# A one-column activation ahead of table loads, and rows of means and scales stored straight from their columns

## The chip, the core and the metric

The kernel runs on one core of a Trainium2 chip. The metric is device microseconds of one execution, as the median of three runs. Besides its timed runs a kernel has one execution taken by the hardware profiler; all rows below are from that one.

## The reference

One sequence of S = 2048 rows and D = 512 columns, 32 heads of 16, F = 1376, all in float32. `xn` is the layernorm of x; A is a linear attention, B a token mixer with an MLP, and the output gates the one with the other:

```
xn = layernorm(x)
q, k, v = xn @ wqkv                       # 32 heads
phi(t) = where(t > 0, t + 1, exp(t)) + 1e-6
kv = sum_s phi(k) v ;  z = sum_s phi(k)
s  = (phi(q) kv / (phi(q) z + 1e-6)) @ wo
h  = gelu(layernorm(xn) @ w1)
hs = [shift +1, -1, +2, -2 of the quarters of h] @ w2
x1 = xn + hs
B  = x1 + gelu(layernorm(x1) @ w3) @ w4
out = x + s * silu(B)
```

## The kernel before

**Tiling.** Rows go in 16 tiles of 128 (`NT`), or 4 blocks of 512 (`NQ` blocks of `QT` = 4 tiles). Matrix products are made in float32r with each operand split into a rounded part and a rest (tiles that end in h and l), so one product is three matmuls. Many products are made by a scheme of seven products of half matrices (`seven`, `keys_queries`, the pairs `p`, `u`, `pb`, `pe`, `pa`, `gf`), which needs sums of operands before and sums of results after; these are ACT's copies and DVE's additions around every group of matmuls.

**Stages.** First the weights wk, wq and w1 and the 16 tiles of x and of its transpose xt are loaded. For each block, means and variances of the rows are taken from x (BATCH_NORM_STATS2 and BATCH_NORM_AGGREGATE into the columns of `mv1`), keys and queries are projected, features of keys are multiplied with x (`gram`, the products g into G), and the mixer's first product h = w1 times u (`mix1`), u being xt less the mean of each row, is scaled by a row factor (`au`) and goes through gelu. Then come w2, the MLP with w3 and w4 in pairs of 128-column slices (tiles `w_`, `f_`, `gf`, `p`, `pb`), and at the end the queries' features against the attention's matrix (`pbs`, with query tiles in pairs q0/q1 to q14/q15), silu, the gating and the store.

**Rows of means and scales.** The mean and the factor of a row stand in columns, one row of x per partition. `make_u` and `mix1` need them along the free axis, on all partitions. `spread` brings them there: TensorE transposes 128x4 numbers into a PSUM bank (`cb` for means, `ab` for scales), ACT copies the 4x128 result (`cr`, `ar`), SP stores it as four rows of 512 bytes into a row in DRAM (`mrow`, `arow`), and a later DMA reads 512 numbers of that row back to all 128 partitions (`um` in `make_u`, `abc` in `join_a`). It runs seven times: four times for scales, three times for means.

**What sets the order.** Every operation is first only recorded (`Plan.add`), with the engine, a duration and what it reads and writes. `Plan.emit` then issues them one at a time: on each engine it chooses among the operations whose inputs are planned by due time, and puts in estimates for table loads (`TABLE`), DMA landings (`RATE`, by kind of transfer) and buffers that come free. A table of pairs at the end of the program, `SOONER`, moves the due times of single operations by quarters of a microsecond. The emitted order is fixed in the program; what the chip then waits for is set by semaphores. A buffer's next user waits for those who used it last.

**Tables on ACT.** Exp, gelu and silu each need their own table of the ACT engine. When an activation with another table than the last follows, the compiler puts an ACT_TABLE_LOAD in front of it. `Plan.act` (L170) knows the three tables by index, and `emit` adds `TABLE` to the planned start where the index changes.

**Queues.** SP issues the loads and the plain stores, in the order in which the planner emitted them; an SP instruction that waits for a semaphore holds all that stand behind it. POOL issues the DMAs that add into their target (`gather`).

**Names that the steps touch.** `w1m` is the product of ones with the sum of w1's rows (`center`, read from `w1ml`), from which DVE takes the centred weights `w_s`, which ACT rounds into `w_0h`, the operand of the first h. `kt` is DVE's sum over a key bank; `qsum` is a later product in the same bank. `turn_q` makes `pq` (ACT, Exp) from queries; `up_pair` makes the MLP's `gf` from its banks (`pb`, `pe`, `pa`) over the copies `p` and `u` (in the orders below `f_..a` are gelu of gf or of a bank, rounded, `f_..t` and `f_..s` the rounded sums of them, `w_2_0h` the rounded sums of a pair of w3). `xr` are the rows of x which the last tiles are gated into; `q14d` and `q15d` the last two query tiles in DRAM, `q14t` and `q15t` the same read back.

Of the kernel before, what the change touches and what calls it, by code (L numbers as in the profile page):

```python
# [8 lines left out]
F32 = mybir.dt.float32  # L9
# [5 lines left out]
P = 128  # L15
# [11 lines left out]
class Tile:  # L27


    def __init__(self, plan, tag, name, dtype, width, rows=P):  # L30
        self.plan, self.tag, self.name, self.dtype, self.width, self.rows = plan, tag, name, dtype, width, rows
        self.ap = None
        self.log = []
        self.left = 0
        self.end = 0.0
        self.psum = tag in plan.psum
        self.early = plan.early
# [45 lines left out]
class Op:  # L83
    __slots__ = ("eng", "busy", "lat", "emit", "pre", "post", "tiles", "opens", "two", "table", "patience", "soon", "loads",
                 "nom", "due", "ready", "at", "end", "mb", "order", "rate", "tail")


class Plan:
# [9 lines left out]
    def add(self, eng, busy, lat, reads, writes, emit, two=False, table=None, mb=0.0):  # L98
# [3 lines left out]
        op.order = len(self.ops)  # L102
        op.patience, op.soon, op.rate, op.tail = self.patience, False, 0.0, 0.0
        op.loads = any(isinstance(v, View) and v.tile.tag != "dram" for v in writes)
# [29 lines left out]

    last_pe = None

    def soon(self, op):
# [21 lines left out]
    def act(self, out, src, func, scale=1.0, bias=None, total=None):  # L159
# [11 lines left out]

        self.add("ACT", lat - .1, lat, [src, scale, bias], [out] + ([] if total is None else [total]), emit, table=table)

# [48 lines left out]
    def gather(self, out, src, share=1.0, kind="gather"):  # L222
# [3 lines left out]
    RATE = {"load": 2.93, "fetch": 3.3, "half": 4.27, "row": 4.23, "turn": 5.4, "store": 2.45,  # L226
            "gather": 5.73, "quarter": 6.42}

# [9 lines left out]
    DMA0 = 2.2  # L238
    TABLE = 1.41
    TAIL = {"row": .95}  # L240
# [33 lines left out]
    def backward(self):  # L274
        for op in reversed(self.ops):
            if op.eng != "PE":
                for o in op.post:
                    op.due = min(op.due, o.due - self.GAP[o.eng] - (6.0 + op.mb * 4 if op.mb else op.lat))

    def emit(self, first, lead, reserve, window, ahead, table=()):  # L280
        self.deadlines(first)
# [14 lines left out]
        under = [0.0] * 8, [0.0] * 8  # L296
        table = 0
        done = set()
        slip = 0.0
        left = len(ops)  # L300
        while left:
# [5 lines left out]
            for e, cands in avail.items():  # L307
                picks = []
                low = INF
                for op in cands:  # L310
# [7 lines left out]
                    if op.table is not None and op.table != table:  # L318
                        s = max(s, free[e] + self.TABLE)
                    ok = True  # L320
# [24 lines left out]
                    if op.table is not None and op.table != table and op.due + slip < s:  # L345
                        q = s - self.TABLE
                    picks.append((q, s, op))
# [35 lines left out]
            for t in op.tiles:  # L383
                t.left -= 1
                t.end = max(t.end, op.end)
                if not t.left and t.tag in slots:
                    insort(slots[t.tag], (t.end, t.slot))
            for o in op.post:
                flow = o.pre[op]
# [17 lines left out]
def linear_attn_gated_by_mixer(  # L407
# [231 lines left out]

    def spread(name, src, b, row):  # L640

        ps = pl.new("mm", f"{name}b{b}", F32, 512)[:QT, :P]
        pl.transpose(ps, src, ident.all)
        t = pl.new("p", f"{name}r{b}", F32, PIECE)[:QT, :P]
        pl.act(t, ps, AF.Copy)
        pl.store(row.via(lambda ap: ap.rearrange("o (j p) -> (o j) p", p=P)), t)

    def spread_a(b):
        spread("a", au[:, b * QT:(b + 1) * QT], b, arow[:, EDGE + b * BT:EDGE + (b + 1) * BT])

    def spread_m(b):
        spread("c", means(mv1, b * QT, (b + 1) * QT), b, mrow[:, b * BT:(b + 1) * BT])

# [964 lines left out]
    for b in range(NQ):  # L1618
# [82 lines left out]
    SOONER = (  # L1701
# [5 lines left out]
    )  # L1707
# [39 lines left out]
```

## Time and profile before

| | us |
|---|---|
| runs | 508.28, 509.31, 509.06 |
| median of the runs | 509.06 |
| the profiled execution | 507.67 |
| its span, from first to last instruction | 505.9 |

| in the profiled execution | |
|---|---|
| operations recorded on the five engines and their queues | 9830 instructions |
| ACT's instructions | 756, of them 26 ACT_TABLE_LOAD and 7 copies of 4x128 |
| PE's matmuls | 3287, of them 7 transposes of a spread |
| DVE, POOL | 945 and 157 instructions |
| DMA | 90895 packets, 115.67 MB |

A row of the profile's timeline reads: start (us), duration (us), engine, line of the kernel, operation, out<-in by the program's names, shapes, and in brackets the time for which the engine stood before it, with the instruction that ended the wait. A row that ends in x3 stands for three such instructions in a run. In the view of waits a row is: engine, what waited, `<-` its releaser; then the total us, how many, and the longest. In the view by groups, numbers behind the bar are total busy us, mean ns of one, and then idle us before the group, with its releasers. The planner's times and the program's order can't be read as times of the chip.

### The profile page before, as it was taken

Reading aid. Unit: us, or ns where it says so; the run is one execution under the profiler, and the core shown is the slowest. Engines: PE = TensorE matmul, PEld = TensorE weight load, DVE = VectorE, ACT = ScalarE, POOL = GpSimd, SP = SyncE. Lnnn points to the kernel's source line nnn. Section 1 sums busy time; section 2 is a strip of 40 time slices with the busy share of each in tenths; the row PEclk is TensorE's granted clock in tenths of the full one; section 3 lists DMA queues with packets and bytes.
Section 4 is the critical chain, followed back from the end, with each engine's and each line's share of the span. In section 5 each row is a group of like instructions: output and inputs, shape, how many; then the busy total and the mean of one; then the engine's idle time right before and its main releaser. Section 6 shows DMA issues by size and latency. Waiting matters only on the chain.

```text
span 505.9 us, 9830 instructions
## 1 busy us (share of the span) xinstructions
PE 496.0 (98%) x3287; PEld 450.9 (89%) x3287; DVE 439.6 (87%) x945; ACT 375.4 (74%) x756; POOL 110.0 (22%) x157
## 2 busy tenths in 40 slices
PE   8999999999999999999999999999998999999996
PEld 6676878898888888898999989999998999999996
DVE  5899999999699995999999997987878869999464
ACT  5899689666797785967767688857588767997551
POOL 2178303363235222021000020300030300031100
PEclk9999999999999999999999999999999999999999
DMA  7957957359994799889785979998799799899905
GB/s 255 356 127 207 314 180 189 62 123 284 269 336 107 227 293 231 265 215 315 260 261 175 317 249 307 225 227 233 226 230 292 160 235 257 258 232 272 245 3 126
DMA packets 90895, 115.67 MB, mean 229 GB/s; under 512 B 8800, under 2 KB 50044, under 8 KB 90844
## 3 DMA queue, kind: packets, MB, share of 16 engines
q1 hardware_dynamic: 78668, 98.00, 60.8%
q0 software_dynamic: 12176, 17.04, 20.4%
q8 instruction: 26, 0.43, 0.3%
q14 instruction: 25, 0.20, 0.1%
HBM read 73.70 MB, written 32.91 MB: 211 GB/s over the span
## 4 chain that ended last, share of the span: by engine, by line
PE 89%; ACT 6%; DMA 3%; DVE 1%; issue 1%; SPq 1%; ACTq 0%
PE a L148 15%; PE pb L148 11%; PE h L148 9%; PE g L148 7%; PE pbk L148 7%; PE acc L148 6%; PE pe L148 6%; PE pbs L148 4%; PE pbm L148 4%; PE pek L148 3%; PE uc L148 3%; PE pa L148 3%; PE pes L148 2%; PE pem L148 2%; PE pak L148 2%; DMA x<-in_x 1%
## 5 line engine op out<-in xcount | busy, mean ns | idle before, releaser
L224 POOL DMA_DIRECT2D th<-in_x x14 | 15.5, 1392 | 169.6 <-DMA w_t<-w4t 59.8
L170 ACT ACT_TABLE_LOAD x26 | 33.4, 1283 | 4.4 <-issue 1.8
L224 POOL DMA_DIRECT2D e<-x1d x12 | 14.4, 1248 | 58.3 <-DMA q8d<-q8z 20.5
L224 POOL DMA_DIRECT2D o<-x x16 | 14.0, 892 | 43.3 <-DVE o L192 30.9
L170 ACT ACTIVATE gf<-gf 128x256 f32<-128x256 f32 (+1 forms) x48 | 21.8, 466 | 0.5
L224 POOL DMA_DIRECT2D zacc<-kr x16 | 14.2, 887 | 36.0 <-DMA zacc<-kr 20.9
L616 POOL TENSOR_TENSOR rs<-w,nhalf 128x4 f32<-128x4 f32 (+2 forms) x10 | 10.1, 1006 | 34.4 <-DVE w L197 24.4
L170 ACT ACTIVATE ht<-ht 128x512 f32<-128x512 f32 x16 | 9.6, 626 | 7.1 <-DVE ht L192 6.8
L170 ACT ACTIVATE p<-pb 128x256 f32<-128x256 f32 x20 | 7.6, 378 | 9.2 <-PE pb L148 9.2
L610 DVE BATCH_NORM_STATS2 st<-o 128x6 f32<-128x512 f32 x16 | 10.8, 684 | 3.2 <-DMA o<-x 3.2
L192 DVE TENSOR_TENSOR gf<-pa,p 128x256 f32<-128x256 f32 x20 | 8.4, 418 | 6.0 <-PE pa L148 4.0
L192 DVE TENSOR_TENSOR th<-th,so 128x512 f32<-128x512 f32 (+1 forms) x17 | 10.7, 655 | 2.7 <-ACT th L170 2.7
L192 DVE TENSOR_TENSOR e<-a,e 128x512 f32<-128x512 f32 (+1 forms) x12 | 7.6, 662 | 6.2 <-PE a L148 6.2
L170 ACT ACTIVATE x<-x,nm,rs 128x512 f32<-128x512 f32 x16 | 12.8, 808 | 0.0
L202 DVE SCALAR_TENSOR_TENSOR kr<-kt,kr 128x512 f32<-128x512 f32 x16 | 10.9, 686 | 2.1 <-ACT kt L170 2.0
L170 ACT ACTIVATE p<-pe 128x256 f32<-128x256 f32 x20 | 7.7, 384 | 6.2 <-PE pe L148 6.1
L202 DVE SCALAR_TENSOR_TENSOR pq<-pq,qr 128x512 f32<-128x512 f32 x12 | 8.1, 687 | 4.4 <-ACT pq L170 4.4
L170 ACT ACTIVATE y<-o,nm,rs 128x512 f32<-128x512 f32 x16 | 11.9, 807 | 0.0
L170 ACT ACTIVATE th<-e 128x512 f32<-128x512 f32 (+1 forms) x12 | 7.1, 611 | 6.4 <-DVE e L192 6.3
L192 DVE TENSOR_TENSOR gf<-u,pe 128x256 f32<-128x256 f32 x20 | 8.2, 408 | 3.9 <-PE pe L148 2.0
L192 DVE TENSOR_TENSOR ht<-h,abc 128x512 f32<-128x512 f32 x16 | 11.0, 686 | 0.4 <-PE h L148 0.3
L202 DVE SCALAR_TENSOR_TENSOR pq<-pq,rd 128x512 f32<-128x512 f32 x16 | 10.5, 670 | 0.0
(1820 smaller groups left out, 2370.3 us busy)
## 6 DMA issues: line engine op xcount, KB each, us to landing
w_s<-in_w SPq DMA_DIRECT2D x34, 256.0 KB, 5.0
w_t<-w4t SPq DMA_DIRECT2D x26, 256.0 KB, 5.3
w_b<-w4d SPq DMA_DIRECT2D x24, 256.0 KB, 4.5
x<-in_x SPq DMA_DIRECT2D x16, 256.0 KB, 4.8
zacc<-kr POOLq DMA_DIRECT2D x16, 256.0 KB, 4.6
o<-x POOLq DMA_DIRECT2D x16, 256.0 KB, 5.5
x1d<-o SPq DMA_DIRECT2D x16, 256.0 KB, 3.9
xt<-in_xt SPq DMA_DIRECT2D x15, 256.0 KB, 5.6
```

The lines of the kernel that those rows point to most:

```text
L148: lambda: nc.tensor.matmul(out.get(), lhs.get(), rhs.get(), start=start, stop=stop, skip_group_check=more))
L170: nc.scalar.activation(out.get(), src.get(), func, scale=get(scale), **kw)
L192: self.vec(eng, out, [a, b], lambda: self.e(eng).tensor_tensor(out.get(), a.get(), b.get(), op=op), True)
L202: lambda: self.nc.vector.scalar_tensor_tensor(out.get(), a.get(), get(s), b.get(), op0=op0, op1=op1),
L224: lambda: self.nc.gpsimd.dma_start(out.get(), get(src), accum_op=ALU.add))
L610: pl.add("DVE", .62, .69, [xv], [st], lambda: nc.vector.bn_stats(st.get(), xv.get()))
L616: lambda: g.tensor_tensor(out.get(), src.get(), nh.get(), op=ALU.pow))
```

## The change

Three things are changed.

A load of a table may now be followed by an activation of one column. `Plan.act` gives every operation that needs a table a second way to emit: `warm`, an activation with the same function from a constant column `tiny` (128x1) into a tile `scr` that nobody reads. `emit` issues it directly ahead of the operation if that operation changes the table and `meets` says that its inputs and the former users of its buffers lie on more than one engine besides ACT. The compiler then puts the table load ahead of the one-column activation, which waits for nothing. The planner counts `EXTRA` for it.

`spread` no longer transposes. One DMA on SP's queue stores the 128x4 columns as they stand, number by number, to their 512 places in `arow` or `mrow`; the planner's rate for this kind is `cells`. The transposes, ACT's copies and the four-row stores go.

The table `SOONER` has other entries, and with the planner's new costs most of the program has a new order.

```
 class Plan:
...
+    scr = None
...
-        self.add("ACT", lat - .1, lat, [src, scale, bias], [out] + ([] if total is None else [total]), emit, table=table)
+        op = self.add("ACT", lat - .1, lat, [src, scale, bias], [out] + ([] if total is None else [total]), emit,
+                      table=table)
+        if table is not None:
+            op.warm = lambda: nc.scalar.activation(self.scr[1].get(), self.scr[0].get(), func)
...
-            "gather": 5.73, "quarter": 6.42}
+            "gather": 5.73, "cells": 500.0, "quarter": 6.42}
...
-    TABLE = 1.41
+    TABLE, EXTRA = 1.41, .22
...
+    def meets(self, op, slots, users):
+
+        e = {o.eng for o in op.pre}
+        n = Counter()
+        for t in op.tiles:
+            if t.ap is None and t.tag in slots and n[t.tag] < len(slots[t.tag]):
+                e |= users.get((t.tag, slots[t.tag][n[t.tag]][1]), set())
+                n[t.tag] += 1
+        return len(e - {"ACT"}) > 1
...
                     if op.table is not None and op.table != table:
-                        s = max(s, free[e] + self.TABLE)
+                        s = max(s, free[e] + self.TABLE + self.EXTRA * self.meets(op, slots, users))
...
+            if op.table is None or op.table == table or not self.meets(op, slots, users):
+                op.warm = None
...
+            if op.warm:
+                op.warm()
             op.emit()
...
+    pl.scr = tiny.all, fixed("scr", 1).all
...
-    def spread(name, src, b, row):
-
-        ps = pl.new("mm", f"{name}b{b}", F32, 512)[:QT, :P]
-        pl.transpose(ps, src, ident.all)
-        t = pl.new("p", f"{name}r{b}", F32, PIECE)[:QT, :P]
-        pl.act(t, ps, AF.Copy)
-        pl.store(row.via(lambda ap: ap.rearrange("o (j p) -> (o j) p", p=P)), t)
+    def spread(src, row):
+
+        pl.move("SP", row, src, "cells", P * QT * 4 / 1e6, [src], [row], lambda: nc.sync.dma_start(
+            row.get().rearrange("o (j p) -> p (o j)", p=P), src.get()))
...
     SOONER = (
-        23, 4, 35, 8, 49, 4, 55, 2, 61, 4, 131, 3, 132, -6, 143, 2, 181, 8, 183, 4, 211, 2, 256, 64, 273, -4,
...
+        35, 32, 132, 6, 143, 4, 155, 2, 181, 3, 183, 6, 201, 16, 256, 64, 321, 36, 330, 64, 353, 2, 393, -16,
...
```

In the new program ACT has 25 table loads (26 before), 14 of them ahead of a one-column activation; PE has seven transposes fewer; SP's queue has seven stores of cells in place of the seven stores of rows.

**The first table load at 378.94 us**, on ACT, in the MLP between two pairs of slices. `pq` are features of queries (the second of a pair is Exp), `p_2` the copies of a bank for which PE waits; the others are named above. Before:

```order
L170 ACTIVATE gf_6_5346<-pb_1_5224 128x256 [waits PE_49]
L170 ACTIVATE f_1a_5378<-pb_1_5224 128x256 [waits PE_49]
L170 ACT_TABLE_LOAD [waits DVE_49]
L170 ACTIVATE pq_5406<-qv_5073,rs_92 128x4x4x32 [waits Activation_49]
L170 ACTIVATE pq_5415<-qv_5079,rs_92 128x4x4x32 [waits PE_49]
L170 ACTIVATE f_1th<-sf_1b 128x512 [waits DMAHW1_49,PE_49]
L170 ACTIVATE f_1sh<-sf_1a 128x512
L170 ACTIVATE p_2_5443<-pb_2_5399 128x256 [waits PE_49]
```

Now:

```order
L172 ACTIVATE w_2_1h<-w_2_fb 128x512 [waits DVE_49]
L172 ACTIVATE f_1a_5360<-pb_1_5201 128x256 [waits DVE_49,PE_49]
L172 ACTIVATE gf_6_5328<-pb_1_5201 128x256 [waits DMAHW1_49]
L172 ACTIVATE gf_6_5328<-gf_6_5328 128x256 [waits Activation_49]
L177 ACT_TABLE_LOAD
L177 ACTIVATE scr<-tiny 128x1
L172 ACTIVATE pq_5399<-qv_5072,rs_93 128x4x4x32 [waits DVE_49]
L172 ACTIVATE f_1th<-sf_1b 128x512 [waits DVE_49,PE_49]
L172 ACTIVATE f_1sh<-sf_1a 128x512 [waits DVE_49,PE_49]
L172 ACTIVATE p_2_5428<-pb_2_5388 128x256 [waits PE_49]
L172 ACTIVATE p_2_5433<-pe_2_5414 128x256 [waits PE_49]
```

The load has lost its wait for DVE, which now stands at pq; a one-column activation is between them, a copy `w_2_1h` stands a few rows ahead, and one pq instead of two comes ahead of p_2.

**The next load, at 386.30 us**, on ACT, back from Exp to gelu. Before:

```order
L170 ACTIVATE yb122h<-y_1t 128x512 [waits DVE_49]
L170 ACTIVATE w_2_0h<-w_2_fa 128x512 [waits PE_49]
L170 ACTIVATE u_2_5473<-pb_2_5399 128x256 [waits PE_49]
L170 ACT_TABLE_LOAD [waits DMAHW5_49,DVE_49]
L170 ACTIVATE f_2a_5505<-gf_7_5496 128x256 [waits PE_49]
L170 ACTIVATE gf_7_5496<-gf_7_5496 128x256 [waits DMAHW1_49,DMASW0_49,Activation_49]
L170 ACTIVATE f_2a_5525<-pb_2_5399 128x256 [waits DMAHW4_49,PE_49]
L170 ACTIVATE gf_7_5496<-pb_2_5399 128x256
```

Now:

```order
L172 ACTIVATE qr_5439<-qv_5164,rs_93 128x4x4x32 [waits DMAHW1_49,Activation_49]
L172 ACTIVATE pq_5449<-qv_5164,rs_93 128x4x4x32 [waits DVE_49]
L172 ACTIVATE u_2_5462<-pb_2_5388 128x256 [waits PE_49]
L172 ACTIVATE yb122h<-y_1t 128x512 [waits DMAHW4_49]
L172 ACTIVATE w_2_0h<-w_2_fa 128x512 [waits Activation_49]
L172 ACT_TABLE_LOAD [waits DMAHW0_49]
L172 ACTIVATE gf_2_5472<-gf_2_5472 128x256 [waits DVE_49]
L172 ACTIVATE f_2a_5514<-gf_2_5472 128x256 [waits DMAHW4_49]
L172 ACTIVATE f_2a_5522<-gf_7_5492 128x256 [waits DVE_49]
L172 ACTIVATE gf_2_5472<-gf_2_5472 128x256 [waits Activation_49]
```

The load waited for DVE and for a transfer; now it waits for a transfer (DMAHW0) alone and the wait for DVE is at the gelu behind it, which is that of gf_2 in place of gf_7. There is no one-column activation here. One qr and one pq stand ahead of u_2.

**Ahead of the first h**, on ACT, among features of queries (qr, qe) and rounded copies (u_, kq_, w1mh), up to w1's centred weights (w_0h, w_1h). Before:

```order
L170 ACTIVATE qe_572<-qt_348,ns_94 128x4x4x32
L170 ACTIVATE qr_579<-qt_504,rs_92 128x4x4x32
L170 ACTIVATE qe_572<-qe_572 128x512 [waits Activation_49]
L170 ACTIVATE qe_593<-qt_504,ns_94 128x4x4x32
L170 ACTIVATE qr_602<-qt_583,rs_92 128x4x4x32 [waits DVE_49]
L170 ACTIVATE u_0h<-xt_0_365 128x512
L170 ACTIVATE qe_593<-qe_593 128x512 [waits Activation_49]
L170 ACTIVATE kq_0h<-kq_0_496 128x512
L170 ACTIVATE w_0h<-w_s_206 128x512 [waits DVE_49]
L170 ACTIVATE w_1h<-w_s_265 128x512 [waits DVE_49]
```

Now:

```order
L172 ACTIVATE qr_562<-qt_405,rs_93 128x4x4x32
L172 ACTIVATE w1mh<-w1t 128x512 [waits DMASW2_49]
L172 ACTIVATE qe_578<-qt_392,ns_95 128x4x4x32
L172 ACTIVATE qe_587<-qt_451,ns_95 128x4x4x32
L172 ACTIVATE qe_578<-qe_578 128x512 [waits Activation_49]
L172 ACTIVATE u_0h<-xt_0_364 128x512 [waits DVE_49]
L172 ACTIVATE qe_587<-qe_587 128x512 [waits Activation_49]
L172 ACTIVATE w_0h<-w_s_258 128x512 [waits DVE_49]
L172 ACTIVATE w_1h<-w_s_288 128x512 [waits DVE_49]
L172 ACTIVATE qr_626<-qt_612,rs_93 128x4x4x32 [waits DVE_49]
```

`kq_0h` no longer stands ahead of w_0h, and there is one qr fewer; w_0h still waits for DVE alone.

More of the change, by code (lines that the diff above doesn't have):

```diff
@@ L1 @@
 from bisect import insort
+from collections import Counter
 from contextlib import ExitStack
@@ L35, in __init__ @@
         self.end = 0.0
-        self.psum = tag in plan.psum
+        self.psum, self.engs = tag in plan.psum, set()
         self.early = plan.early
@@ L84 @@
     __slots__ = ("eng", "busy", "lat", "emit", "pre", "post", "tiles", "opens", "two", "table", "patience", "soon", "loads",
-                 "nom", "due", "ready", "at", "end", "mb", "order", "rate", "tail")
+                 "nom", "due", "ready", "at", "end", "mb", "order", "rate", "tail", "warm")
 class Plan:
@@ L102, in add @@
         op.order = len(self.ops)
-        op.patience, op.soon, op.rate, op.tail = self.patience, False, 0.0, 0.0
+        op.patience, op.soon, op.rate, op.tail, op.warm = self.patience, False, 0.0, 0.0, None
         op.loads = any(isinstance(v, View) and v.tile.tag != "dram" for v in writes)
@@ L297, in emit @@
         table = 0
+        users = {}
         done = set()
@@ L345, in emit @@
                     if op.table is not None and op.table != table and op.due + slip < s:
-                        q = s - self.TABLE
+                        q = s - self.TABLE - self.EXTRA
                     picks.append((q, s, op))
@@ L385, in emit @@
                 t.end = max(t.end, op.end)
+                t.engs.add(e)
                 if not t.left and t.tag in slots:
                     insort(slots[t.tag], (t.end, t.slot))
+                    users[t.tag, t.slot] = t.engs
             for o in op.post:
@@ L638, in linear_attn_gated_by_mixer @@
     ABC = {}
-    def spread(name, src, b, row):
-        ps = pl.new("mm", f"{name}b{b}", F32, 512)[:QT, :P]
-        pl.transpose(ps, src, ident.all)
-        t = pl.new("p", f"{name}r{b}", F32, PIECE)[:QT, :P]
-        pl.act(t, ps, AF.Copy)
-        pl.store(row.via(lambda ap: ap.rearrange("o (j p) -> (o j) p", p=P)), t)
+    def spread(src, row):
+        pl.move("SP", row, src, "cells", P * QT * 4 / 1e6, [src], [row], lambda: nc.sync.dma_start(
+            row.get().rearrange("o (j p) -> p (o j)", p=P), src.get()))
     def spread_a(b):
-        spread("a", au[:, b * QT:(b + 1) * QT], b, arow[:, EDGE + b * BT:EDGE + (b + 1) * BT])
+        spread(au[:, b * QT:(b + 1) * QT], arow[:, EDGE + b * BT:EDGE + (b + 1) * BT])
     def spread_m(b):
-        spread("c", means(mv1, b * QT, (b + 1) * QT), b, mrow[:, b * BT:(b + 1) * BT])
+        spread(means(mv1, b * QT, (b + 1) * QT), mrow[:, b * BT:(b + 1) * BT])
     def join_a(b):
```

8 rows, old and new, of the table SOONER are left out of this document.

## The prediction

> **What bounds the kernel now.** I read the page first: which engine is full, and what the chain of work that ended last consists of.
>
> ```profile
> PE 496.0 (98%) x3287; PEld 450.9 (89%) x3287; DVE 439.6 (87%) x945; ACT 375.4 (74%) x756; POOL 110.0 (22%) x157
> PE 89%; ACT 6%; DMA 3%; DVE 1%; issue 1%; SPq 1%; ACTq 0%
> ```
>
> TensorE is busy for 98% of the span and makes up 89% of the chain. Time can only come from fewer matmuls or from places where PE stands. The view of waits, kept to PE, names those places with their releasers.
>
> ```profile
> PE h L148 <- ACT w_0h L170: 1.3, 1, 1.3
> PE warm L148 <- POOL ones L523: 1.0, 1, 1.0
> PE pb L148 <- ACT p L170: 1.0, 1, 1.0
> PE k L148 <- DMA wk_s<-in_wqkv: 0.9, 1, 0.9
> PE qsum L148 <- DVE kt L202: 0.8, 1, 0.8
> PE a L148 <- ACT gf L170: 0.6, 1, 0.6
> ```
>
> Six waits, 5.6 us together. The first, third and last end on ACT: at 44.55 us, 382.93 us and 389.06 us. The last two are in the third quarter of the kernel. The timeline of ACT there, then of DVE and PE:
>
> ```profile
> 378.94 1.28 ACT L170 ACT_TABLE_LOAD   x1 [1.33 <-DVE sf_1a L192]
> 380.23 1.34 ACT L170 ACTIVATE pq<-qv,rs 128x512 f32<-128x512 f32 x2
> ...
> 382.52 0.36 ACT L170 ACTIVATE p<-pb 128x256 f32<-128x256 f32 x1
> ...
> 386.30 1.28 ACT L170 ACT_TABLE_LOAD   x1 [1.83 <-issue]
> ...
> 388.63 0.38 ACT L170 ACTIVATE gf<-pb 128x256 f32<-128x256 f32 x1
> ```
>
> ```profile
> 385.81 0.41 DVE L192 TENSOR_TENSOR gf<-pb,p 128x256 f32<-128x256 f32 x1
> ```
>
> ```profile
> 382.93 0.38 PE L148 MATMUL pb<-yt22h,w_s0h 128*128 128x256 f32 x1 [1.02 <-ACT p L170]
> ...
> 389.06 0.36 PE L148 MATMUL a<-yb112h,w_lh 128*96 128x256 f32 x1 [0.61 <-ACT gf L170]
> ```
>
> Both PE waits have the same cause. The table load carries the waits of the activation behind it, so it stands idle first (1.33 us; 1.83 us, until DVE's gf is done at 385.81 + 0.41 = 386.22) and loads only then, for 1.28 us. Everything queued behind it on ACT is late: the copy p at 382.52, for which PE stood 1.02 us, and the gelu gf at 388.63, for which it stood 0.61 us. How common is that?
>
> ```profile
> L170 ACT ACT_TABLE_LOAD x26 | 33.4, 1283 | 4.4 <-issue 1.8 <-DVE sf_1a L192 1.3 <-PEq L1738 0.8
> ```
>
> Of 26 loads, these two hold 3.1 of the 4.4 us of idle time (0.8 is the start of the program). The other loads stand directly behind other ACT work; there is nothing to take from them.
>
> **The change, part by part.**
>
> *Loads ahead of the wait.* The new order has 25 loads, 14 of them with the one-column activation behind them. At the first place the load now has no wait and the activation pq takes DVE's. It can begin when ACT falls idle, 378.94 - 1.33 = 377.61, and end at 378.89, with pq right behind: 380.23 becomes about 379.1, or 1.1 us earlier. Only one pq instead of two stands before p, another 0.6 us. p then comes about 1.7 us sooner, or 1.2 us after the 0.5 us that one newly moved copy (w_2_1h) costs ahead of the load. PE waited 1.02, so the wait is gone. At the second place the planner saw only one engine to wait for and adds no activation, but the gelu that needs the table is now gf_2; the wait on DVE moved from the load to it, and the load keeps a wait on one transfer only. I take that transfer as landed, since gf_2's contents have already been written into the tile by DVE. The load then hides in the 1.83 us, and the 0.61 us go as well. Together 1.63 us, no more, because PE has no other wait there; if the second load is still held, 1.02; if neither is freed, 0.
>
> The Trainium skill, in "ScalarE: Activation LUTs", section "What ACT_TABLE_LOAD costs", gives a switch as 1283 ns of load and about 1380 ns of drain. By that rule a load begun at 377.61 would be done no earlier than 380.27, the first place would gain nothing from it, and the whole sum would come to 1.2 us instead of 2.2. The trace disagrees: the activation behind the load at 378.94 starts 1.29 us later, with no drain between.
>
> *Fourteen activations.* Nearest row: the 4x128 copy of a spread, which also is an ACT instruction of minimal width.
>
> ```profile
> 29.60 0.25 ACT L170 ACTIVATE cr<-cb 4x128 f32<-4x128 f32 x1
> 29.76 0.61 ACT L170 ACTIVATE k2h<-kr 128x512 fp32r<-128x512 f32 x1
> ```
>
> It lasts 0.25 us and the next one starts after 0.16. So 14 cost 2.2 to 3.5 us of ACT, against seven such copies taken away (1.1 us). ACT is idle for a quarter of the span and PE waits for it in three places only, which is the cover; without it all of 3.5 us would reach PE. I take 0.2 us lost, bounds 0 and 3.5.
>
> *Spreads without TensorE.* Seven transposes leave PE (four of scales, three of means). Their price shows in the starts of the neighbours:
>
> ```profile
> 28.89 0.40 PE L148 MATMUL g<-k0h,x0h 128*128 128x512 f32 x1
> 29.12 0.27 PE L153 MATMUL cb<-ident,mv 128*4 128x128 f32 x1
> 29.15 0.48 PE L148 MATMUL g<-k0l,x0h 128*128 128x512 f32 x1
> 29.46 0.39 PE L148 MATMUL g<-k0h,x0l 128*128 128x512 f32 x1
> ```
>
> Matmuls of 512 columns start 0.23 us apart (28.89 to 29.12). From 29.12 to 29.46 a transpose and one matmul take 0.34, so a transpose costs 0.11 us. Four of the seven lie after 44.55, where PE is full: 0.44 us. The other three are part of the front, below.
>
> *Stores of cells.* In place of four rows of 512 bytes each store now moves 512 numbers of four bytes. How that lands, the trace does not show. What it may cost:
>
> ```profile
> 27.53 0.37 DVE L611 BATCH_NORM_AGGREGATE mv<-st 128x2 f32<-128x6 f32 x4
> ```
>
> ```profile
> 29.88 0.27 SPq L216 DMA_DIRECT2D mrow<-cr  x1
> 31.58 0.33 SPq L220 DMA_DIRECT2D um<-mrow  x1
> ```
>
> ```profile
> DMA to landing us min/median/max: 3.2/3.2/3.2
> ```
>
> ```profile
> 38.09 0.68 DVE L192 TENSOR_TENSOR xt<-xt,um 128x512 f32<-128x512 f32 x1
> ```
>
> ```profile
> q1 hardware_dynamic: 78668, 98.00, 60.8%
> ```
>
> The means are ready at 27.9. The old store went at 29.88 and the read back waited for it until 31.58, 1.7 us; its data land 3.2 us after its issue (the view of tile um), at 34.8; the first user starts at 38.09. The new store needs no transpose and can go at 27.9. It may therefore take 38.09 - 3.2 - 27.9 = 7.0 us to land, or 5.3 us more than now, before anyone is late. A packet of this queue takes 0.608 x 16 x 505.9 / 78668 = 63 ns of one engine on average; 512 of them over 16 engines are 2.0 us, over four engines 8.0 us, on one 32 us. I take 2.0: hidden. Bounds: 0, and 1.7 + 32 - 7.0 = 27 us late.
>
> The Trainium skill speaks against these stores: "DMA: Bandwidth & Descriptors", section "Specifications", says that below 512 bytes the engine reads, modifies and writes, and its section "Bandwidth" measures about 10.5 ns for each packet. An estimate from that page is 5.4 us for 512 packets and 2 us of fixed cost, 0.4 us beyond the slack, so the sum would be 1.8 us instead of 2.2. No run here shows a four-byte store.
>
> *The front, up to the first product of the mixer.*
>
> ```profile
> 42.44 0.39 PE L148 MATMUL w1m<-w1ml,onesr 128*128 128x512 f32 x1
> ...
> 44.55 0.49 PE L148 MATMUL h<-u_0h,w_0h 128*128 128x512 f32 x1 [1.26 <-ACT w_0h L170]
> ```
>
> ```profile
> 43.37 0.61 ACT L170 ACTIVATE kq_0h<-kq 128x512 fp32r<-128x512 f32 x1
> 43.89 0.61 ACT L170 ACTIVATE w_0h<-w_s 128x512 fp32r<-128x512 f32 x1
> ```
>
> ```profile
> 43.03 1.88 DVE L202 SCALAR_TENSOR_TENSOR w_s<-w1m,w_s 128x512 f32<-128x512 f32 x3
> ```
>
> From the second w1m product (ends 42.83) over DVE's w_s and ACT's w_0h to h are 1.7 us, and two matmuls cover 0.46. The new order keeps this chain and two matmuls of cover, so the wait of 1.26 stays. What can move is w1m itself: by three transposes (0.33 us), and by the qsum wait (0.81 us), since the new order frees that bank first. ACT is no hindrance (three copies of 0.16, one kq_0h and one qr less before w_0h), but w1ml on DVE stands behind three subtractions and half a sum more, about 2.2 us of DVE work. I take 0.5 us gained, bounds 0 and 1.1.
>
> *The order elsewhere.* After 45 us PE waits for nothing but the two loads, so a new order can only lose there. I take 0.2 us lost, bounds 0 and the 2.1 us of the rival on the last pair.
>
> Sum: 1.63 - 0.2 + 0.44 + 0.5 - 0.2 = 2.2 us. The profiled execution took 507.67 (a span of 505.9 and 1.8 around it), which becomes 505.5; the median of the three runs lies 1.39 above it, 509.06, and becomes **506.9**.
>
> **The rivals.**
>
> *Neither load is freed* (the change does not do what it says): the activation behind the load waits as late as the load did, and both PE waits stay. For it: one load still carries a transfer's wait. Against it: the first has none. 506.9 + 1.6 = 508.5.
>
> *ACT becomes the bound*: 14 activations stand where ACT has no idle time before its loads (1.3 us in 24 loads), each pushes the copies behind it by up to 0.25 us, and PE's covers are as tight as at 382.93. It decides from the point where a copy that PE waits for comes later than its last cover matmul. All 14 on PE's path: 506.9 + 3.3 = 510.2, slower than before. Against it: ACT's quarter of idle time lies between the loads and absorbs most of it.
>
> *The last pair of query tiles comes late.*
>
> ```profile
> 473.21 3.92 SPq L220 DMA_DIRECT2D q15t<-q15d  x4
> 478.01 0.40 SPq L212 DMA_DIRECT2D xr<-in_x  x1
> ```
>
> ```profile
> DMA to landing us min/median/max: 5.9/5.9/5.9
> ```
>
> ```profile
> 483.23 0.28 PE L148 MATMUL pbs<-m_b11h,q14h 128*128 128x256 f32 x1
> ```
>
> In the new order all eight reads of q14t and q15t stand behind both loads of xr, the second of which waits for ACT. If it goes at 478.01 again, eight issues (3.9 us for four now) and a landing of 5.9 us (the view of tile q15t, second fence) bring the queries to about 487.8, and ACT's copy to 488.4; the new order wants pbs 2.6 us nearer to the end, at about 486.3. A wait of 2.1 us: 509.0. Against it: the second xr stands earlier, and its tile may be free.
>
> *The cells land late*: over four engines, 1.7 + 8.0 - 7.0 = 2.7 us at the front, 509.6; on one engine 27 us, 534. It decides once a store takes over 7.0 us. Against it: 128 partitions are offered where the old store had four rows.
>
> **How the numbers follow.** Forecast 0.62; neither load freed 0.08; ACT the bound 0.14; last pair 0.08; cells 0.08. What this kernel's measurement tells from no change is about 0.2%, or 1.0 us. Faster by more (below 508.0) is the forecast and the better part of the first rival, 0.64; within it the rest of that rival, the last pair and half of the cells, 0.16; slower 0.20. Low end: the upper bounds of the gains (1.63 + 0.44 + 1.1 = 3.2) and the lowest of the three runs (0.8 below the median) give 505.1, taken as 505.0. High end: ACT the bound, 510.2.
>
> **What would show it.** Right: no PE wait on p or gf between 375 and 390 us; a load there followed by a 128x1 activation and then by idle time; no 4x128 rows; PE's count at 3280; um landing before the first xt subtraction. Wrong: a PE wait of over 0.3 us after 45 us that was not there; xt or ht waiting for a DMA of um or abc; pbs waiting for q14h near 486; ACT copies behind the loads named as PE's releasers.

## The result

| | before | after |
|---|---|---|
| median of 6 runs, us | 508.74 | 516.49 |
| lowest to highest | 507.91 to 509.31 | 513.58 to 519.36 |
| profiled execution (its span) | 507.67 (505.9) | 514.23 (512.5) |

The ratio after to before is 1.0148, with a 95% interval of 1.0109 to 1.0186: slower by 1.5%, where 506.9 had been forecast. A ratio here compares means and leaves out runs that lie more than 1.5% above the fastest of their kernel, while a median is that of all runs, so the two can part where the runs spread widely; both are given. That the spread of after is four times that of before (5.8 us against 1.4) belongs to the finding.

First the page of the changed kernel, its busy engines and its chain:

```profile
PE 498.8 (97%) x3280; PEld 450.2 (88%) x3280; DVE 440.9 (86%) x945; ACT 374.1 (73%) x762; POOL 104.1 (20%) x157
PE 82%; DMA 11%; DVE 4%; ACT 2%; issue 1%; SPq 1%; DVEq 0%; ACTq 0%
```

PE's count is 3280 as expected, but its share of the chain fell from 89% to 82%, and DMA's rose from 3% to 11%. The view of waits of PE names the new places; the waits on p and gf at 383 and 389 us are gone from it:

```profile
PE pbk L150 <- ACT kq_1h L172: 2.5, 1, 2.5
PE h L150 <- ACT w_0h L172: 1.3, 1, 1.3
PE pbk L150 <- DVE p5k L197: 1.2, 1, 1.2
PE warm L150 <- POOL ones L546: 1.0, 1, 1.0
PE g L150 <- DVE k3l L207: 1.0, 1, 1.0
```

The chain of waits in order of time shows where it begins:

```profile
24.78 0.30 DVE mv L634 x4
...
25.10 9.52 DMA mrow<-mv
...
34.63 4.32 DMA um<-mrow
...
38.98 0.69 DVE xt L197
```

The means are ready at 25.08, earlier than before, and the store of cells goes at once. It takes 9.52 us to land. The read back waits for it on SP until 34.63 and takes 4.32 us, and the first subtraction starts at 38.98 instead of 38.09. DVE stood for it 2.4 us, which the view of tile mrow names (`DVE xt L197: 2.4, 1`); behind that stand k3l, for which PE waits 1.0 us, and w1ml and w_s, so that the first h comes at 45.96 instead of 44.55.

While the cells land, other transfers slow down. The same stretch of time by windows, before, after, and in a kernel that has the changed order with cheaper stores (the block stores told below; busy time of PE, PEld, DVE, ACT and POOL with the number of instructions, then granted clock, DMA share, GB/s):

```profile
26.00:46.00 20.00, 18.74 (x83) 14.48 (x82) 18.91 (x45) 20.00 (x38) 15.84 (x26) 1.00 0.55 135
```

```profile
26.00:46.00 20.00, 17.44 (x73) 13.02 (x71) 16.88 (x39) 18.05 (x33) 6.63 (x16) 1.00 0.96 87
```

```profile
26.00:46.00 20.00, 18.77 (x82) 14.78 (x81) 19.20 (x43) 19.98 (x37) 14.71 (x24) 1.00 0.60 163
```

The DMA engines are busy for 96% of these 20 us instead of 55%, and move 87 GB/s instead of 135; with block stores it is 60% and 163 GB/s. A high DMA share at a low rate is read here as engines that wait on something; on what, the trace does not show. The issues in this window show whom it hits: the accumulating zacc<-kr lands after 3.3 us before and 9.9 us now, the stores of query features pqd<-qr after 2.1 and 10.2 us (medians; with block stores 5.5 and 2.1). First before, then after:

```profile
pqd<-qr SPq DMA_DIRECT2D x3, 256.0 KB, 2.1
pqd<-qe POOLq DMA_DIRECT2D x3, 256.0 KB, 7.1
zacc<-kr POOLq DMA_DIRECT2D x2, 256.0 KB, 3.3
```

```profile
pqd<-qr SPq DMA_DIRECT2D x3, 256.0 KB, 10.2
zacc<-kr POOLq DMA_DIRECT2D x2, 256.0 KB, 9.9
arow<-au SPq DMA_DIRECT2D x2, 2.0 KB, 10.5
```

Three accumulating pqd<-qe of this window before are absent after: they come later. The longest new wait is at 70 us. The timeline of ACT and of PE there:

```profile
69.51 0.63 ACT L172 ACTIVATE w_b21h<-w_s 128x512 fp32r<-128x512 f32 x1 [3.19 <-DMA w_s<-in_w]
70.05 0.61 ACT L172 ACTIVATE kq_1h<-kq 128x512 fp32r<-128x512 f32 x1
```

```profile
70.71 0.50 PE L150 MATMUL pbk<-kq_1h,u_3h 128*128 128x512 f32 x1 [2.46 <-ACT kq_1h L172]
...
72.71 0.63 PE L150 MATMUL pek<-kq_0l,us_0h 128*128 128x512 f32 x1
73.14 0.63 PE L150 MATMUL pek<-kq_0h,us_0l 128*128 128x512 f32 x1
```

A load of w2, issued at 60.03 us, takes 9.45 us; ACT's rounding of it waits 3.19 us, kq_1h is queued behind, and PE stands 2.46 us. The load itself is not slower for the cells. With block stores in the same order the same load takes 10.1 us, but it is issued 7.8 us earlier. The waits of SP's queue and its rows, and the landing of the load, in the changed kernel:

```profile
SPq L225 <- DMA arow<-au: 4.8, 1, 4.8
46.15 0.32 SPq L225 DMA_DIRECT2D abc<-arow  x1
60.03 0.66 SPq L217 DMA_DIRECT2D w_s<-in_w  x1
w_s<-in_w SPq DMA_DIRECT2D x1, 256.0 KB, 9.5
```

The same with block stores, where abc waits for no store:

```profile
40.19 0.38 SPq L225 DMA_DIRECT2D abc<-arow  x1
52.26 0.65 SPq L217 DMA_DIRECT2D w_s<-in_w  x1
w_s<-in_w SPq DMA_DIRECT2D x1, 256.0 KB, 10.1
```

SP issues in order. Its read back abc stands until the scales' cells have landed (two stores, issued from 35.05 us on, that take 10.5 us), and all that is behind it in the queue goes later: abc by 6.0 us, the w2 load by 7.8, of which 2.2 us of waiting for a slow pqd<-qr are a part. The cells thus reach PE through a queue that their reader holds up. This is read from the two traces; no run moves the read back alone. At 147 us it is the other way, a slow transfer: an accumulating o<-x, issued while two stores of cells land, takes 9.25 us in the chain (9.6 in the median of two there, 5.6 with block stores), and PE waits 1.2 us for p5k behind it.

After the long wait PE pays a second time: from 72.31 to 75.70 matmuls start 0.43 us apart instead of 0.23. The windows give a granted clock of 0.50 from 72.4 to 75.7 us, 0.83 between 66 and 76. Eight matmuls lose 0.2 us each, 1.5 us on top of the wait (3.39 us for eight starts, which take 1.84 at 0.23).

At the place of the first held load the forecast holds:

```profile
386.09 1.28 ACT L177 ACT_TABLE_LOAD   x1
387.38 0.20 ACT L177 ACTIVATE scr<-tiny 128x1 f32<-128x1 f32 x1
387.49 0.71 ACT L172 ACTIVATE pq<-qv,rs 128x512 f32<-128x512 f32 x1
```

### The profile page after: what moved, and what is told of

The parts are those of the page before. It is cut to its first block, busy times and chain, and to the rows that moved or that the text cites. A ratio compares the mean times of both kernels' runs of the same rounds, so it can differ in the third digit from the quotient of the medians.

```text
span 512.5 us, 9824 instructions
## 1 busy us (share of the span) xinstructions
PE 498.8 (97%) x3280; PEld 450.2 (88%) x3280; DVE 440.9 (86%) x945; ACT 374.1 (73%) x762; POOL 104.1 (20%) x157
## 4 chain that ended last, share of the span: by engine, by line
PE 82%; DMA 11%; DVE 4%; ACT 2%; issue 1%; SPq 1%; DVEq 0%; ACTq 0%
PE a L150 15%; PE pb L150 10%; PE h L150 9%; PE g L150 6%; PE acc L150 6%; PE pbk L150 5%; PE pe L150 5%; PE pbs L150 4%; PE pbm L150 4%; PE uc L150 3%; PE pek L150 3%; PE pa L150 2%; PE pes L150 2%; PE pem L150 2%; DMA mrow<-mv 2%; DMA w_s<-in_w 2%
## 5 line engine op out<-in xcount | busy, mean ns | idle before, releaser
L639 POOL TENSOR_TENSOR rs<-w,nhalf 128x4 f32<-128x4 f32 (+2 forms) x10 | 10.5, 1054 | 43.7 <-DVE w L202 28.1
L172 ACT ACTIVATE x<-x,nm,rs 128x512 f32<-128x512 f32 x16 | 12.9, 806 | 0.8 <-DVE nm L207 0.8
L197 DVE TENSOR_TENSOR th<-th,so 128x512 f32<-128x512 f32 (+1 forms) x17 | 10.7, 651 | 2.2 <-ACT th L172 2.2
L197 DVE TENSOR_TENSOR gf<-u,pe 128x256 f32<-128x256 f32 x20 | 8.3, 415 | 5.0 <-PE pe L150 4.5
L197 DVE TENSOR_TENSOR ht<-h,abc 128x512 f32<-128x512 f32 x16 | 10.7, 678 | 2.1 <-PE h L150 1.1
L197 DVE TENSOR_TENSOR gf<-pa,p 128x256 f32<-128x256 f32 x20 | 8.3, 416 | 4.5 <-PE pa L150 1.9
L197 DVE TENSOR_TENSOR e<-a,e 128x512 f32<-128x512 f32 (+1 forms) x12 | 7.6, 657 | 4.9 <-PE a L150 4.9
L1383 DVE TENSOR_REDUCE den<-qz 128x32 f32<-128x512 f32 x16 | 10.7, 678 | 0.1
```

Source lines behind the costliest of these rows:

```text
L172: nc.scalar.activation(out.get(), src.get(), func, scale=get(scale), **kw)
L197: self.vec(eng, out, [a, b], lambda: self.e(eng).tensor_tensor(out.get(), a.get(), b.get(), op=op), True)
L639: lambda: g.tensor_tensor(out.get(), src.get(), nh.get(), op=ALU.pow))
L1383: pl.add("DVE", .6, .68, [t], [den], lambda: nc.vector.tensor_reduce(den.get(), t.get().rearrange("p (h d) -> p h d", d=DH), axis=AX.X, op ...
```

## The experiments

**Is it the stores or the order?** One run puts cells' stores into the order before; one gives the changed order cheaper stores; one gives it the old spread.

Before with stores of cells (transposes and copies still run, unread):

```
-        pl.store(row.via(lambda ap: ap.rearrange("o (j p) -> (o j) p", p=P)), t)
+        dst = row.via(lambda ap: ap.rearrange("o (j p) -> p (o j)", p=P))
+        pl.move("SP", dst, t, "store", ..., [t], [dst], lambda: nc.sync.dma_start(dst.get(), src.get()))
```

> The kernel before, its order unchanged, the transposes and copies still there but unread; only the seven stores write single numbers (512 of four bytes each) straight from the columns. Theory C (the cells' stores cost the time: they take 8 to 12 us to land, hold the DMA engines meanwhile, and so delay um and every other transfer): the first store goes at about 29.9, lands near 39.5, um near 43.5 instead of 34.8, the first subtraction on DVE waits some 5 us, PE stands for about as long ahead of the first h and runs at a lower clock after it; 513 to 520 us. Theory O (the new order is at fault, the stores are harmless): 508 to 509.5, no wait on um.

533.51 us (531.32 to 536.46), ratio 1.0514 (1.0466 to 1.0562). The stores alone cost the old order more than the new one, beyond even theory C's range. They land later there, after 11.4 to 16.8 us as far as shown, against 7.6 to 10.6 in the changed kernel, and three of them are issued within 2.1 us (85.8 to 87.9); how much of the difference that makes was not tried. PE's waits:

```profile
PE g L148 <- DVE x3l L192: 5.4, 1, 5.4
PE pbm L148 <- ACT p1m L170: 5.4, 1, 5.4
PE pem L148 <- ACT hs30h L170: 3.9, 1, 3.9
PE pbm L148 <- DVE ht L192: 3.9, 1, 3.9
```

The changed order with block stores, 128 packets of 16 bytes or 64 of 32 (each row holds 512 numbers, but not the reference's: the scales in another arrangement, and in place of 512 means the means and variances of half the partitions, so the wrong numbers meet the rows of x):

```
-            row.get().rearrange("o (j p) -> p (o j)", p=P), src.get()))
+            row.get().rearrange("o (p j) -> p (o j)", j=w),
+            mv1.ap[:P // 2, 2 * b * QT:2 * (b + 1) * QT] if wide else src.get()))
```

> The changed kernel, its order unchanged, each of the seven stores writes its 512 numbers in 128 packets of 16 bytes (scales) or 64 packets of 32 bytes (means), to the same row but in another arrangement, so the row holds other numbers than the reference's. Theory C: the store lands in 2.5 to 4 us, no wait on um, no wait of PE over 1.3 us between 45 and 160 us; 506 to 508.5 us. Theory O: the waits of PE at 61, 71 and 147 us stay; 513 to 517.

504.85 us (504.38 to 505.07), ratio 0.9938 (0.9923 to 0.9953). The same order, the same seven DMAs at the same places, other packets: 11.6 us less than the changed kernel by the medians (10.7 by the ratios), and the spread is gone as well. That is theory C, and 1.2 us below its range, though the first store lands in 4.6 us and not in 2.5 to 4. The first um lands in 3.3, and PE's waits behind the start are two:

```profile
PE h L150 <- ACT w_0h L172: 1.2, 1, 1.2
...
PE q L150 <- DVE kt L207: 0.3, 1, 0.3
```

Since both kernels issue PE's matmuls in one order, their profiles (512.5 and 502.7 us) can be compared matmul by matmul. The changed kernel is 2.2 us behind at the first h (45.96 against 43.73), 5.9 at the end of the long wait (70.71 against 64.81), 7.6 at the end of the slow matmuls (75.70 against 68.08), 9.0 at 146.72 (against 137.74) and 9.8 at the end.

The changed kernel with the transposes and row stores back (entries of SOONER at the same operations, the planner decides anew):

```
+        pl.transpose(ps, src, ident.all)
+        pl.act(t, ps, AF.Copy)
-        pl.move("SP", row, src, "cells", ...)
+        pl.store(row.via(lambda ap: ap.rearrange("o (j p) -> (o j) p", p=P)), t)
```

> The changed kernel with the old spread (transpose, copy, four rows), the entries of its table at the same operations as before, one-column activations kept; the order follows the planner anew. Theory C: 506 to 508.5 us. Theory O: 512 or more, with waits of PE before 160 us that the kernel before does not have.

509.42 us (507.33 to 514.36, 10 runs), ratio 1.0025 (0.9997 to 1.0054). Inconclusive: it falls between both theories. It has new waits of PE (on p1m 1.0 us at 126 us, on gf and u 0.6 to 0.7 us near 350 us); the transposes make another order than the one the table was set for, which may be why.

**What are the one-column activations worth?** First the changed kernel without them:

```
-            if op.warm:
-                op.warm()
```

> The changed kernel, its order unchanged, without the one-column activations. Theory L (they free the held loads as forecast, at almost no price elsewhere): 0.5 to 2 us slower than the changed kernel, waits of PE on ACT near 380 to 395 us come back. Theory A (14 more instructions on ACT cost more than they free): 1 to 3 us faster than the changed kernel. The waits before 160 us stay in both.

515.25 us (513.47 to 516.29), ratio 1.0140 (1.0116 to 1.0165) against 1.0148 with them: below what such scattered runs can tell. The waits near 380 to 395 us did not come back, against theory L; the new order alone had removed them there. So the same edit was made where nothing hides it, in the changed order with block stores, and the activations alone were put into the order before, ahead of all 25 changes of table:

> The changed kernel with block stores (128 packets of 16 or 64 of 32 bytes, the row's numbers in another arrangement), order unchanged, without the one-column activations. Theory N (the new order alone has taken the waits away, the activations are worth nothing): within 0.6 us of the same kernel with them, 504.3 to 505.4 us. Theory L: 1 to 2 us more, 505.9 to 506.9.

> The kernel before, its order unchanged, with a one-column activation ahead of every operation that changes the table (25). Theory L (a load without waits hides in the idle time): PE's waits on ACT's p at 383 and gf at 389 us are gone, 0.7 to 1.6 us faster than before. Theory A (the activations cost ACT what they free): 25 x 0.11 us = 2.8 us of ACT, of which up to 1.5 reach PE; same as before or up to 1.5 slower.

In the changed order with block stores: 506.26 us without (504.87 to 508.27), 504.85 with them, ratios 0.9959 (0.9945 to 0.9973) and 0.9938. In the order before: 507.32 us (506.21 to 508.06), ratio 0.9975 (0.9964 to 0.9986). In the order before the two waits of PE are gone, and the load no longer stands:

```profile
378.71 1.28 ACT L176 ACT_TABLE_LOAD   x1
380.01 0.20 ACT L176 ACTIVATE scr<-tiny 128x1 f32<-128x1 f32 x1
380.12 1.32 ACT L171 ACTIVATE pq<-qv,rs 128x512 f32<-128x512 f32 x2
```

```profile
L176 ACT ACT_TABLE_LOAD x25 | 32.1, 1283 | 0.4
L176 ACT ACTIVATE scr<-tiny 128x1 f32<-128x1 f32 x25 | 5.1, 203 | 0.3
```

The 25 loads behind the first one now stand 0.4 us together, and one activation takes 0.20 us, with the next starting 0.11 after it. PE's order is that of the kernel before, so the gain can be seen in place. The matmul pb at 375.93 before starts at 377.02 here, 1.1 us later (0.8 of it at the first h already, 45.33 against 44.55); pb behind the first place starts at 382.84 instead of 382.93, and a behind the second at 388.15 instead of 389.06. Less those 1.1 us the load at 378.71 is where the forecast put it, at 377.61. This is theory L. It is less clear in the changed order. The median without the activations is in theory L's range too, but the two ratios are 0.21% apart, and the uncertainty of such a difference, by their intervals, is as large; the lowest of these runs is as fast as those with them. This kernel, the old one with the activations and nothing else, computes the whole reference and beats both kernels compared here.

**What makes a store of cells slow?** The changed kernel with block stores gets, behind each, a second store of the same 512 numbers one by one to memory that nobody reads. The numbers stand side by side, or each in its own 512 or 64 bytes (`APART` 1, 128, 16):

```
+            nc.sync.dma_start(far.ap.rearrange("o (j p k) -> p (o j) k", p=P, k=APART)[:, :, 0], src.get())
```

> The changed kernel with block stores for the reader, and behind each a store of the same 512 numbers one by one to a row that nobody reads. Theory M (a cells' store holds up other transfers, whoever waits for it): the unread store lands 8 to 11 us after its issue, um and the accumulating DMAs land late, 508 to 514 us. Theory W (only the reader's wait counts): 504.8 to 506, the issue of seven more DMAs.

> As the kernel with the unread store, but each of the 512 numbers goes to its own 512 bytes. Theory S (single writes to the same short stretch of memory stand in line for each other): the unread store lands in 3 to 5 us, 504.8 to 506.5 us. Theory P (every packet has its price wherever it goes): as the near one.

> As the kernel with the unread store of single numbers, now 64 bytes apart (adjacent: 4 bytes; far: 512 bytes). If stretches of 512 bytes are what the writes share, it lands in 8 us or more and the time is above 508; if 64 bytes are enough, it lands in 3 to 5 us, 504.8 to 506.5 us.

Side by side: 513.40 us (506.79 to 516.19; the profiled execution 514.71), ratio 1.0018 (0.9993 to 1.0043). 512 bytes apart: 504.99 (504.53 to 507.63), ratio 0.9939 (0.9920 to 0.9959). 64 bytes apart: 506.88 (506.37 to 507.48), ratio 0.9965 (0.9951 to 0.9979). The times to landing (last column, us) decide; the tile is called far in all three. Side by side, then 512 bytes apart, then 64 bytes apart:

```profile
um<-mrow SPq DMA_DIRECT2D x3, 256.0 KB, 10.0
far1False<-au SPq DMA_DIRECT2D x1, 2.0 KB, 12.9
far2True<-mv SPq DMA_DIRECT2D x1, 2.0 KB, 8.6
```

```profile
um<-mrow SPq DMA_DIRECT2D x3, 256.0 KB, 6.7
far1False<-au SPq DMA_DIRECT2D x1, 2.0 KB, 2.8
far2True<-mv SPq DMA_DIRECT2D x1, 2.0 KB, 3.4
```

```profile
um<-mrow SPq DMA_DIRECT2D x3, 256.0 KB, 6.5
far1False<-au SPq DMA_DIRECT2D x1, 2.0 KB, 2.9
far2True<-mv SPq DMA_DIRECT2D x1, 2.0 KB, 3.2
```

All unread stores that show a landing took 8.6 to 12.9 us side by side and 2.8 to 5.1 us apart, and the three pages count the same 95352 DMA packets. So it is neither the number of packets nor their size alone; it is that so many of them write into the same short stretch of memory. A short stretch alone isn't enough either: the 128 packets of 16 bytes stand side by side too and land in 1.4 to 3.7 us in the kernel with block stores alone. What happens in the memory or the DMA engines, no run shows. And nobody reads the slow ones: theory W falls, theory M holds. With unread stores of adjacent cells um's read takes 10.0 us (median of three) instead of 6.7 and 6.5, and PE waits 2.0 us (for k3l at 43 us) and 2.8 us (for p5k at 146 us). The run at 64 bytes is 1.9 us above that at 512 in the median and 0.4 above its expected range; its waits of PE lie at the start and near 350 us, not at the stores, and what they come from was not followed up.

**What is the rest worth?** The order before with the activations and with block stores in place of transposes, copies and row stores (rows in another arrangement again):

```
+        for op in pl.ops[first:]:
+            op.emit, op.warm = lambda: None, None
```

> The order before, with a one-column activation ahead of every change of table, the seven transposes and copies left out and block stores in their place (the row's numbers in another arrangement). Against the same without the block stores (507.3 us) it prices the spreads: forecast 0.44 us for four transposes past 45 us and 0.33 for three at the front, 506.5 us. If the new order is worth nothing besides, 504.9, as the changed kernel with block stores.

506.86 us (505.74 to 507.30), ratio 0.9959 (0.9944 to 0.9974). As a ladder of ratios: activations 0.9975, block stores besides 0.9959, the new order besides 0.9938. The steps are 0.25%, 0.16% and 0.21%, or 1.3, 0.8 and 1.1 us; the uncertainty of a difference of two such ratios is about 0.2%, so the last two are not told from nothing (and the last step also goes from 25 activations to 14).

**Can cheap stores be had with the right numbers?** Block stores whose arrangement the readers undo, by reading um and abc with a stride of 16 bytes:

```
-        pl.tt(XT[b, c], XT[b, c], m, ALU.subtract)
+        v = XT[b, c].via(lambda ap: ap.rearrange("q (j p) -> q j p", p=P))
+        pl.tt(v, v, m.via(lambda ap: ap.rearrange("q (p j) -> q j p", j=QT)), ALU.subtract)
```

> The changed kernel in its order, computing the whole reference: means and scales are kept in columns side by side, each store writes 128 packets of 16 bytes, so that the row in memory holds the four numbers of a partition next to each other; the readers on DVE take um and abc with a stride of 16 bytes, and two to three stores of two packets each bring the neighbours' scales for the shifts. Theory C: as the kernel with block stores, 504.4 to 506.5 us, no wait on um. Rival R (DVE's strided reads are slower, 28 of them): each product or subtraction on DVE takes over 0.69 us, waits of PE on DVE's xt or ht in 38 to 190 us, 508 or more.

513.46 us (512.00 to 513.75), ratio 1.0086 (1.0072 to 1.0101): rival R. The groups of DVE, before and in this kernel (busy us, mean ns of one):

```profile
L192 DVE TENSOR_TENSOR ht<-h,abc 128x512 f32<-128x512 f32 x16 | 11.0, 686 | 0.4 <-PE h L148 0.3
L192 DVE TENSOR_TENSOR xt<-xt,um 128x512 f32<-128x512 f32 x12 | 7.9, 683 | 0.0
```

```profile
L197 DVE TENSOR_TENSOR ht<-h,abc 128x512 f32<-128x512 f32 x16 | 16.8, 1061 | 1.0 <-PE h L150 1.0
L197 DVE TENSOR_TENSOR xt<-xt,um 128x512 f32<-128x512 f32 x12 | 12.6, 1086 | 0.0
```

Each of the 28 instructions takes 0.38 to 0.40 us more, 10.5 us of DVE in all, in stages where DVE has no idle time to give (from 26 to 76 us it was busy for 48.8 of 50 us before). DVE waits neither for um's nor for abc's read. What the additional small stores of this kernel cost was not separated.

## Why the prediction was wrong

**The step that failed** is "I take 2.0: hidden", the landing of a store of cells. It measured 9.52 us, against a point of 7.0 us from which it had been said to decide. Its signs of being wrong came with it: xt waited for um, and PE had new waits. By the prediction's own formula that is 9.5 - 7.0 = 2.5 us late, and DVE's wait on um measured 2.4. The formula was right, and the size was taken from the wrong row. That the numbers agree so well is luck in part: the means were ready at 25.1 and not at 27.9, DVE stood ready for xt at 36.6 and not at 38.09, and um took 4.3 us and not 3.2, which happens to leave a slack of 7.2 us. The mean time of a packet of the queue, 63 ns, is an average over packets of other sizes and says nothing of writes that share a short stretch of memory; the bounds, 0 and 27 us, showed that this row carried no weight, and 2.0, which lies in the slack, was still taken.

**The rival was under-priced too.** Cells that land late were priced at 2.7 us, the delay of the one reader. That covers the front: of the 9.8 us between the two profiles 2.2 had arisen at the first h. Measured, the seven stores cost 11.6 us (516.49 against 504.85). The prediction has no term for the rest: other transfers slow down while the cells land, a read back that waits holds up SP's queue and with it the w2 load, PE waits 2.46 and 1.2 us far from the first h, and its clock is lower after the longest wait.

The Trainium skill, in "DMA: Bandwidth & Descriptors", section "Specifications", has writes under 512 bytes read, modify and write. The estimate made from that page's figure per packet, which the page measured on loads into SBUF, was 7.4 us, nearer to the 9.5 us than the value taken. But four-byte writes 64 bytes apart, which that rule covers as well, land in 2.9 to 5.1 us, so that the estimate came near is no support for it; the price here is that of neighbours, which no figure for a single packet gives.

**What was right.** The loads: 1.63 - 0.2 = 1.4 us forecast, and 1.4 us measured in the old order (508.69 to 507.32; 1.3 by the ratio), where both waits went as described. In the new order the medians are 1.4 us apart as well (506.26 to 504.85; 1.1 by the ratios), but there the waits would have gone at these two places without the activations. With block stores and no activations the profile shows a load held elsewhere for 0.89 us (ahead of th, at 296 us), behind which PE's matmuls are 0.7 us late at 301 us, and a wait of PE of 0.6 us for gf at 350 us. That wait stands in kernels with the activations too (0.4 and 0.6 us with unread cells 512 and 64 bytes apart), so for the new order the agreement is in part luck. *ACT becomes the bound* did not happen: 25 activations cost 5.1 us of ACT and no wait of PE. *The last pair* did not come late: no wait on q14h is in the view. *Neither load is freed* did not happen; the transfer on which the second load still waits had landed.

The spreads without TensorE: 0.77 us forecast (0.44 and the three transposes of the front), 0.8 measured by the ratios, with an uncertainty larger than that (0.5 by the medians, 507.32 to 506.86). The front: h comes at 43.73 with block stores against 44.55, 0.8 us, with the wait of 1.2 us still there as forecast; 0.5 had been taken. The order elsewhere was taken at a loss of 0.2 us; the ladder makes the new order worth about 1.1 us in all, front included, at the edge of what it can tell. Without the cells the sum, 506.9, would have been too high by 2.0 us, of which 0.9 is the kernel before itself (509.06 in the prediction's three runs, 508.18 beside the block stores).

Three small slips had no part in this. The two waits near 383 and 389 us lie at the start of the last quarter, not in the third. For the last pair 486.3 does not come out of its rows: 483.23 + 2.6 is 485.8, which makes that rival's wait 2.6 us and its time 509.5. And the chances beside the 0.64 add up to 0.18 within and 0.18 slower by their own parts, not 0.16 and 0.20.

## What to carry to other kernels

Before a spread by DMA is priced, ask where its packets are written: 512 four-byte writes side by side in memory took 7.6 to 10.6 us to land here and slowed other transfers, and what has to be looked for is a high DMA share at a low rate and the queue that a waiting read back holds up, not only the wait of the reader. An instruction with a constant input ahead of a table change lets the load run while the real user still waits, for 0.1 us of ACT each, and can be added without touching the order. When a cost has bounds of 0 and 27 us and decides from 7 us on, the range has to say so: the row that gave the middle must come from the same pattern of access.

## What the runs showed of the hardware

- 512 four-byte writes landed in 8.6 to 12.9 us when adjacent and in 2.8 to 5.1 us when 64 or 512 bytes apart (the DMA issues of the three kernels with unread cells, as far as they show a landing). Read by the kernel, the adjacent ones took 7.6 to 10.6 us in the changed kernel and 11.4 to 16.8 in the order before.
- After some long waits of PE the granted clock was 0.50 for a while: after 2.0, 2.46, 2.8 and 5.4 us seven to ten matmuls of 512 columns started about 0.43 us apart instead of 0.23, and after 3.9 and 5.4 us in the order before with cells matmuls of 256 columns started 0.21 us apart instead of 0.12. After others (2.2 and 2.3 us in the changed kernel without activations) and after all of 1.8 us and less, past the start, the matmuls kept their pace. So the length alone does not decide; what does was not found. It is one source of the spread: of the changed kernel's runs the fastest, 513.58 us, has a mean granted clock of 0.998 and the slowest, 519.36, one of 0.993.
- DVE's 128x512 products and subtractions of ht and xt took 0.68 to 0.69 us with adjacent operands and 1.06 to 1.09 us where one operand has a stride of 16 bytes.
- The activation behind an ACT_TABLE_LOAD started 1.29 us after the load did, here too (386.09 to 387.38); the one-column activation took 0.20 us and the next started 0.11 us after it.
